# Turning the routed rows of six experts by DMA transposes of two-byte planes, with gates and weight loads moved behind them

## The chip, the cores and the metric

The kernel runs on one core of a Trainium2 chip, as one launch. The metric is the device time of an execution in microseconds, as a median of several runs; lower is better. The kernel before takes 338.1 us (three runs: 337.73, 338.10 and 340.49).

## The reference, cut to what matters

Two layers follow each other, all in float32.

- A gated recurrent attention over 768 steps for 4 batches of 8 heads of width 40. It gives `x`, a matrix of 3072 tokens by 320 features.
- A mixture of 8 experts with one expert per token. `logits = normalize(x) @ normalize(emb).T / tau`; each token goes to its largest logit, and its gate is the softmax share of that logit. Then, for each expert `e` and the tokens sent to it:

```
h = np.maximum(x[mask] @ w1[e], 0.0)                 # 320 -> 1024
out[mask] = gate_w[mask, None] * (h @ w2[e])         # 1024 -> 320
```

`w1` is 8 x 320 x 1024 and `w2` is 8 x 1024 x 320. The change touches only the expert layer, from the point where the token lists of all experts are known.

## The kernel before, in words

The order of the work is written out by hand: every engine takes its instructions in the order of the program, and closures in lists (`todo`, `xps`, `early`) say after which matrix product the next small piece of other work is put into the engines' queues. The DMA queue of SyncE (SP) issues the plain loads and stores in that order too; POOL issues the indirect ones.

**Precision.** Each float32 operand of a matrix product is split into a high and a low part (`xh`/`xl`, `w1h`/`w1l`, `hh`/`hl`, `w2h`/`w2l`), and a product is three matmuls. The last 64 features of `x` stand in one tile `xt`, high parts in partitions 64 to 127 and low parts in 0 to 63.

**The lists.** Attention output rows lie in DRAM as `x_d`, 336 floats a row: 320 features and the gate. The first two experts have special treatment: their first 256 rows each are gathered while attention still runs, and their second 256 rows ("b" in tile names) follow. The other six are sorted by size (`arrange`, line 217) and get lists of at most 448, 448, 384, 384, 320 and 320 rows (`CAPS`). An expert of these six is a pass `e` of the loop at line 1480, `e` from 2 to 7, with `j = e - 2`.

**One pass.** `mm1` (line 366) makes one of 8 blocks of the hidden layer: 8 matmuls into a PSUM tile `ph` (three of them exist), a ReLU on ACT into `hh`, a subtraction on DVE into `hl`. `mm2` (line 385) makes up to 128 output rows: 24 matmuls into a PSUM tile `po` (two exist), multiplied by the gate on DVE into `ob`, and scattered to `out` by an indirect DMA of POOL. For a list that ends in 64 rows, the last block takes 16 matmuls, a copy on ACT and two operations on DVE.

**What a pass prepares for the next one.** While pass `e` computes, pass `e + 1` is made ready:

- `load` (line 166) asks for the seven raw weight pieces, three of `w1` (512, 512 and twice 256 KB) and four of `w2` (320 KB each), on the SP queue. There are seven buffers `raw`, so a load waits until the piece of the expert before it in that buffer is split. All seven are put into the SP queue at the start of the pass.
- `piece` (line 186) splits a raw piece: a copy on ACT, a subtraction on DVE. One piece follows each `mm1` and two follow each `mm2`.
- `gather` (line 313) fetches the rows of the list into `xs`, 128 rows per indirect DMA of POOL, also at the start of the pass (the lists of `j` = 0 and 1 earlier).
- `x_chunk` (line 332) turns the rows. For each of three chunks of 128 features, TensorE transposes the three or four blocks of rows into one PSUM tile `pt`; ACT and DVE split it into `xh`/`xl` or `xt`. The first chunk is turned after the first `mm2`, the other two after the second. For the first of the six lists the three chunks follow the first three `mm2` of the "b" rows.
- `row_gates` (line 316) copies the gates of the list from `xs` at the start of its own pass.

**Before the loop.** The "b" rows go through 16 `mm1` of 256 rows (8 for each of the two experts) and 4 `mm2`. Beside the first of them run the small DVE steps of `arrange` (`ranks`, `places`, `lists`, `beyond`). `where` (line 1440) reads the sorted order into SP registers and puts all seven loads of expert 2 into the queue; `tokens` (line 1448) gathers the first list.

Of the kernel before, what the change touches and what calls it, by code (L numbers as in the profile page):

```python
# [11 lines left out]
F32 = mybir.dt.float32  # L12
# [2 lines left out]
F16 = mybir.dt.float16  # L15
I32 = mybir.dt.int32
U32 = mybir.dt.uint32
AF = mybir.ActivationFunctionType
ALU = mybir.AluOpType
AX = mybir.AxisListType  # L20
# [3 lines left out]
E, F = 8, 1024  # L24
NT = B * S
DM = H * D
P = 128
L = 64
# [6 lines left out]
CAP = 512  # L35
NTT = CAP // P
# [4 lines left out]
NE = 2  # L41
# [4 lines left out]
CAPS = (448, 448, 384, 384, 320, 320)  # L46
TILES = [[slice(a, min(a + P, n)) for a in range(0, n, P)] for n in CAPS]
# [21 lines left out]
def tile_mlstm_moe(  # L69
# [22 lines left out]
    V, G, A, T, SY = nc.vector, nc.gpsimd, nc.scalar, nc.tensor, nc.sync  # L92
# [5 lines left out]

    y_d = dr.tile([S, B * H, D], F32, name="y_d", tag="y_d")
    x_d = dr.tile([NT + 1, XW], F32, name="x_d", tag="x_d")  # L100
    left_d = dr.tile([E, NS, P, 1], I32, name="left_d", tag="left_d")
    oe_d = dr.tile([E, 1], I32, name="oe_d", tag="oe_d")

# [209 lines left out]
    def gather(cols):  # L313
        return gather_rows(lp.tile([P, NTT, XW], F32, name="xs", tag="xs"), cols)

    def row_gates(xs, n):

        gt = mp.tile([P, NTT], F32, name="gt", tag="gt")
        for a in range(0, n, P):
            r = min(P, n - a)  # L320
            V.tensor_copy(gt[0:r, a // P : a // P + 1], xs[0:r, a // P, DM:XC])
        return gt
# [9 lines left out]
    def x_chunk(x, xs, c, w=CAP):  # L332
        xh, xl, xt = x
        pt = pM.tile([P, 512], F32, name="pt", tag="pm")[:, 0:w]
        f = (0, P, DM - P)[c]
        for a in range(0, w, P):
            r = min(P, w - a)
            T.transpose(pt[:, a : a + r], xs[0:r, a // P, f : f + P], ident[0:r, 0:r])  # L338
        if c < 2:
            A.copy(xh[:, c, 0:w], pt)  # L340
            V.tensor_tensor(xl[:, c, 0:w], pt, xh[:, c, 0:w].bitcast(F32), ALU.subtract)
        else:
            A.copy(xt[L:P, 0:w], pt[L:P])
            V.tensor_tensor(xt[0:L, 0:w], pt[L:P], xt[L:P, 0:w].bitcast(F32), ALU.subtract)
# [21 lines left out]
    def mm1(ws, x, xc, f, hs, hc):  # L366
        w1h, w1l, (xh, xl, xt) = ws["w1h"], ws["w1l"], x
        fs = slice(f * P, (f + 1) * P)
        ph = pH.tile([P, 512], F32, name="ph", tag="ph")[:, 0 : xc.stop - xc.start]
        ops = [(w[:, c, fs], xh[:, c, xc]) for c in range(2) for w in (w1h, w1l)]  # L370
        ops += [(w1h[:, c, fs], xl[:, c, xc]) for c in range(2)]
        ops += [(w[:, 2, fs], xt[:, xc]) for w in (w1h, w1l)]
        for i, (lt, rh) in enumerate(ops):
            T.matmul(ph, lt, rh, start=i == 0, stop=i == len(ops) - 1)  # L374
        hh, hl = hs[0][f][:, hc], hs[1][f][:, hc]
        A.activation(hh, ph, AF.Relu)  # L376
        w = hc.stop - hc.start
        m = w - w % P
        V.scalar_tensor_tensor(hl[:, 0:m], ph[:, 0:m], 0.0, hh[:, 0:m].bitcast(F32), ALU.max, ALU.subtract)  # L379
        if m < w:  # L380
            V.scalar_tensor_tensor(
                hs[0][f][:, w : 2 * w - m], ph[:, m:w], 0.0, hh[:, m:w].bitcast(F32), ALU.max, ALU.subtract
            )
# [94 lines left out]
    with ExitStack() as actx:  # L478
# [711 lines left out]
        w_loads, exps = [], {}  # L1190
# [127 lines left out]
        def do(k):  # L1318
            for _ in range(k):
                if todo:  # L1320
                    todo.pop(0)()
# [56 lines left out]
        def first_out(i, po, ob=None):  # L1378
            mm2_out(po, xs_a[:, i // HT, i % HT, DM:XC], ida_v[i], f"a{i}", ob)
# [43 lines left out]

    exps[1]["tiles"](w22[1], 2)
    xs = gather(slots_b)
    todo += [exps[1]["piece"](*p) for p in PIECES2]
    while early:
        work(1, 2)
# [6 lines left out]
    first_outs = [(None, ob0), (None, ob1), (po2,), (po3,)]  # L1435

    gt_b = row_gates(xs, CAP)
    at = []

    def where():  # L1440

        at.extend(
            nc.values_load(order[0:1, j : j + 1], engines=[ET.SP], min_val=0, max_val=E - 1) for j in range(NO)
        )
        exps[2] = load_expert(2, at[0])
        todo[:] += [exps[2]["load"](i) for i in range(7)]

    def tokens():
        nonlocal xs
        xs = gather(ids_v[0])  # L1450

    ranks, places, lists, beyond = arrange(mp)
    todo += ranks + places + [where] + lists + [tokens]
    hs = hidden("b")
    for e in range(NE):
        for f in range(FC):
            mm1(exps[e]["ws"], xp, slice(e * HALF, (e + 1) * HALF), f, hs, slice(e * HALF, (e + 1) * HALF))
            do(3 - e)
            if f % 4 == 1:
                first_out(2 * e + f // 4, *first_outs[2 * e + f // 4])  # L1460
        if e == 0:
            exps[2]["tiles"](wp, 1)
            todo += beyond
    xp = x_tiles(mp, "2", CAP)
    xps = [lambda c=c: x_chunk(xp, xs, c, CAPS[0]) for c in range(3)]
    todo += [exps[2]["piece"](*p) for p in PIECES1]
    for i in range(NE * HT):
        e, a = divmod(i, HT)
        mm2(exps[e]["ws"], hs, slice(i * P, (i + 1) * P), gt_b[:, i : i + 1], slots_b[i], f"b{i}")
        if i == 1:  # L1470
            xs_n = gather(ids_v[1])
        if i == HT - 1:
            exps[2]["tiles"](w22[0], 2)
            todo += [exps[2]["piece"](*p) for p in PIECES2]
        do(3 if i < HT else 4)
        if xps:
            xps.pop(0)()
    while todo:
        do(1)
    for e in range(NE, E):  # L1480
        j = e - NE
        ws, x, w = exps[e]["ws"], xp, slice(0, CAPS[j])
        xps = []
        gt = row_gates(xs, CAPS[j])
        if e + 1 < E:
            exp = exps[e + 1] = load_expert(e + 1, at[j + 1])
            exp["tiles"](wq if e % 2 == 0 else wp, 1)
            exp["tiles"](w22[(e + 1) % 2], 2)
            todo += [exp["load"](i) for i in range(7)]
            todo += [exp["piece"](*p) for p in PIECES1 + PIECES2]  # L1490
            n = CAPS[j + 1]
            xs = gather(ids_v[j + 1]) if j else xs_n
            xp = x_tiles(mp, e + 1, CAP)
            xps = [lambda c=c, xp=xp, xs=xs, n=n: x_chunk(xp, xs, c, n) for c in range(3)]
            do(7)
        hs = hidden(e)
        for f in range(FC):
            mm1(ws, x, w, f, hs, w)
            do(1)
        for i, a in enumerate([0, len(TILES[j]) - 1, *range(1, len(TILES[j]) - 1)]):  # L1500
            t = TILES[j][a]
            mm2(ws, hs, t, gt[0 : t.stop - t.start, a : a + 1], ids_v[j][a], f"{e}_{a}")
            for _ in range(1 + (i == 1)):
                if xps:
                    xps.pop(0)()
            do(2)
        while todo:
            do(1)
        while xps:
            xps.pop(0)()  # L1510
# [209 lines left out]
```

## Time and profile before

| | |
|---|---|
| median of three runs | 338.1 us |
| profiled execution | 339.62 us, of which the span of the trace is 337.9 |
| TensorE (PE) busy | 313.2 us, 93% of the span |
| DVE, ACT, POOL busy | 223.3, 161.6 and 148.7 us |
| share of PE in the chain that ended last | 80% |
| mean granted TensorE clock | 0.968 of full speed |
| PE and clock from 192 to 330 us | busy all 138 us, clock 1.00 |

A matmul's length in the trace overlaps the next one's, so the pace of TensorE is read from the distance of two starts, or from the chain of waits, which gives each group only the time by which it moved the end. A row of the chain is: start, length, engine, names, line, count. In a timeline a row is: start, length, engine, line, operation, what it writes and reads, and in brackets the idle time before it and what ended that. "SPq" is the SP queue, and the time of such a row is that of the issue, not of the transfer. In a table by window, each engine has its busy time in the window with the instruction count, and at the end stand the granted clock, the busy share of the 16 DMA engines and GB/s.

### The profile page before, as it was taken

Reading aid. Unit: us, or ns where it says so; the run is one execution under the profiler, and the core shown is the slowest. Engines: PE = TensorE matmul, PEld = TensorE weight load, DVE = VectorE, ACT = ScalarE, POOL = GpSimd, SP = SyncE. Lnnn points to the kernel's source line nnn. Section 1 sums busy time; section 2 is a strip of 40 time slices with the busy share of each in tenths; the row PEclk is TensorE's granted clock in tenths of the full one; section 3 lists DMA queues with packets and bytes.
Section 4 is the critical chain, followed back from the end, with each engine's and each line's share of the span. In section 5 each row is a group of like instructions: output and inputs, shape, how many; then the busy total and the mean of one; then the engine's idle time right before and its main releaser. Section 6 shows DMA issues by size and latency. Waiting matters only on the chain.

```text
span 337.9 us, 9698 instructions
## 1 busy us (share of the span) xinstructions
PE 313.2 (93%) x3697; PEld 293.4 (87%) x3697; DVE 223.3 (66%) x644; ACT 161.6 (48%) x416; POOL 148.7 (44%) x183
## 2 busy tenths in 40 slices
PE   7859998989988999989699999999999999999992
PEld 3848897888977889989699999999999999999992
DVE  6776787897995679846336594566666684675520
ACT  6584654645654584533144363354454372554310
POOL 7775676667777387232423501250340231322112
PEclk9797999999999799999879999999999999999997
DMA  5896698999996541120871966437348458330001
GB/s 157 296 308 218 200 276 282 261 273 264 283 299 175 180 136 39 23 71 22 243 226 45 296 205 181 127 101 224 108 138 210 125 175 193 94 99 29 21 19 38
DMA packets 31610, 56.24 MB, mean 166 GB/s; under 512 B 6970, under 2 KB 21510, under 8 KB 31554
## 3 DMA queue, kind: packets, MB, share of 16 engines
q1 hardware_dynamic: 28738, 47.08, 47.7%
q0 software_dynamic: 2560, 8.35, 8.3%
q8 instruction: 31, 0.51, 0.6%
q14 instruction: 25, 0.20, 0.2%
q10 hardware_dynamic: 256, 0.10, 0.1%
HBM read 47.51 MB, written 8.39 MB: 165 GB/s over the span
## 4 chain that ended last, share of the span: by engine, by line
PE 80%; DMA 7%; DVE 4%; issue 3%; ACT 2%; another core or an unknown queue 1%; POOL 1%; POOLq 0%; SPq 0%
PE ph L374 28%; PE po L406 17%; PE s L571 5%; PE po_b L406 4%; PE y L652 4%; PE y L663 3%; PE po_a L406 3%; DMA kv_s<-in_kv 3%; PE c L610 3%; PE po L391 3%; PE pt L338 3%; PE pm L729 2%; DMA kq_s<-in_kq 2%; PE px L715 2%; DMA en<-in_emb 1%
## 5 line engine op out<-in xcount | busy, mean ns | idle before, releaser
L425 POOL DMA_INDIRECT out<-ob,ids x20 | 19.7, 985 | 102.7 <-DVE ob L422 86.4
L376 ACT ACTIVATE hh<-ph 128x448 fp32r<-128x448 f32 (+2 forms) x48 | 23.6, 491 | 45.4 <-PE ph L374 24.8
L406 PE MATMUL po<-w2h,hh 128*128 128x320 f32 x128 | 40.3, 314 | 0.0
L406 PE MATMUL po<-w2h,hl 128*128 128x320 f32 x128 | 39.6, 309 | 0.0
L406 PE MATMUL po<-w2l,hh 128*128 128x320 f32 x128 | 39.6, 309 | 0.0
L556 POOL TENSOR_TENSOR uv<-kv_s,u_t 64x328 f32<-64x328 f32 x47 | 34.8, 740 | 7.3 <-DMA kv_s<-in_kv 2.7
L379 DVE SCALAR_TENSOR_TENSOR hl<-ph,hh 128x384 fp32r<-128x384 f32 (+1 forms) x48 | 24.5, 511 | 15.5 <-ACT hh L376 11.8
L374 PE MATMUL ph<-xh,w1h 128*128 128x448 f32 (+2 forms) x96 | 32.1, 337 | 0.0
L571 PE MATMUL s<-kq_s 128*64 128x64 f32 x768 | 29.2, 231 | 3.1 <-DVE w_s L580 1.6
L374 PE MATMUL ph<-xh,w1l 128*128 128x448 f32 (+2 forms) x96 | 32.0, 336 | 0.0
L571 PEld LDWEIGHTS s<-kq_s 128*64 128x64 f32 x768 | 26.8, 145 | 4.7 <-DVE w_s L580 2.5
L195 ACT CAST w1h<-raw 128x512 fp32r<-128x512 f32 x48 | 28.9, 613 | 0.0
L422 DVE TENSOR_SCALAR ob<-po,gt 128x320 f32<-128x320 f32 x16 | 8.8, 551 | 28.9 <-PE po L406 28.9
L198 DVE TENSOR_TENSOR w2l<-raw,w2h 128x320 fp32r<-128x320 f32 x58 | 27.1, 503 | 0.2
L699 POOL TENSOR_TENSOR x<-x,sig 128x320 f32<-128x320 f32 x21 | 18.2, 865 | 17.9 <-DMA kq_s<-in_kq 5.6
L652 PE MATMUL y<-uv,w_s 128*64 128x82 f32 x384 | 25.2, 247 | 0.2 <-issue 0.2
L195 ACT CAST w2h<-raw 128x320 fp32r<-128x320 f32 x62 | 25.2, 458 | 0.1
L374 PE MATMUL ph<-xl,w1h 128*128 128x448 f32 (+2 forms) x96 | 24.5, 336 | 0.0
L198 DVE TENSOR_TENSOR w1l<-raw,w1h 128x512 fp32r<-128x512 f32 x36 | 24.4, 686 | 0.0
L406 PEld LDWEIGHTS po<-w2h,hh 128*128 128x128 f32 x128 | 24.0, 188 | 0.3
L406 PEld LDWEIGHTS po<-w2l,hh 128*128 128x128 f32 x128 | 24.1, 188 | 0.0
L406 PEld LDWEIGHTS po<-w2h,hl 128*128 128x128 f32 x128 | 24.0, 188 | 0.0
(312 smaller groups left out, 921.3 us busy)
## 6 DMA issues: line engine op xcount, KB each, us to landing
raw<-in_w SPq DMA_DIRECT2D x32, 320.0 KB
kv_s<-in_kv SPq DMA_DIRECT2D x24, 324.0 KB
kq_s<-in_kq SPq DMA_DIRECT2D x48, 160.0 KB
raw<-in_w SPq DMA_DIRECT2D x14, 512.0 KB
raw<-in_w SPq DMA_DIRECT2D x18, 256.0 KB
sig<-in_og SPq DMA_DIRECT2D x24, 160.0 KB
x_d<-x SPq DMA_DIRECT2D x24, 160.0 KB
raw<-in_w SPq DMA_DIRECT2D x4, 128.0 KB
```

The source lines that it names most:

```text
L195: A.copy(h, src)
L198: (eng or V).tensor_tensor(lo, src, h.bitcast(F32), ALU.subtract)
L338: T.transpose(pt[:, a : a + r], xs[0:r, a // P, f : f + P], ident[0:r, 0:r])
L374: T.matmul(ph, lt, rh, start=i == 0, stop=i == len(ops) - 1)
L376: A.activation(hh, ph, AF.Relu)
L379: V.scalar_tensor_tensor(hl[:, 0:m], ph[:, 0:m], 0.0, hh[:, 0:m].bitcast(F32), ALU.max, ALU.subtract)
L406: T.matmul(po[0 : ts_.stop - ts_.start, 0:DM], lt[f][:, ts_], rh[:, f], start=k == 0, stop=k == len(ops) - 1)
L425: store = G.indirect_dma_start(out=out, out_offset=bass.IndirectOffsetOnAxis(ap=slots, axis=0), in_=ob, in_offset=None, bounds_check=NT - ...
L556: eng.tensor_tensor(uv[n % NB][rows, :, :, r], list(rows_of(n))[1][rows], u_t[rows, j, b].unsqueeze(3).broadcast_to([L, 2, NP, D1]), ALU.mult,
L571: T.matmul(s[r * L : r * L + L, c, p], k_of(n, odd)[:, a, cs], q_of(n)[:, a, cs], start=True, stop=True,)
L652: T.matmul(yh[c][:, g, :, odd], w_s[n % NB][:, c, 2 * g + odd], uv[n % NB][:, c, 2 * g + odd], start=g + odd == 0, stop=n < B and c == 0, ...
L699: eng.tensor_tensor(x_of(n), x_of(n), sigs[j][:, b].rearrange("p (h d) -> p h d", h=H), ALU.mult)
```

## The change

- `x_chunk` is no longer used for the six lists. A function `turn` makes the steps for one list: `part` copies 128 rows on POOL from `xs` into `halves`, pulling the two 16-bit halves of each float apart into two planes of 384 columns (320 used, the rest zero); `go` copies the gates on DVE, stores the planes to DRAM (`x2_d`, one or two DMAs), and then issues one transposing DMA from `x2_d` into `turned`, where the two halves of a float come to lie side by side again. All these DMAs are on the SP queue.
- `split` makes `xh`, `xl` and `xt` from `turned` with two steps: `rows` (the first 256 features in one ACT copy and one DVE subtraction) and `rest`.
- In pass `e`, `part` and `go` follow one `mm1` each. The loads of the next `w2` come behind `go`, one after each further `mm1` or `mm2`; those of the next `w1` stay at the start of the pass. The splits of `w2` follow the `mm2` only. `rows` and `rest` follow the first and second `mm2`.
- The rows of the list after next are gathered after the first `mm2` of a pass.
- For the first list, the parts follow the "b" `mm1` of the second expert from its second block on, `go` and the `w2` loads come behind, and `rows` and `rest` follow the second and third `mm2`. `where` comes behind `tokens`, and the three `w1` loads are put between the steps of `beyond`.

```diff
+    def turn(xs, j):
+        n, full = CAPS[j], CAPS[j] // P
+        def part(a):
+            r = min(P, n - a * P)
+            G.tensor_copy(halves[0:r, a, :, 0:DM], xs[0:r, a, 0:DM].bitcast(U16).rearrange("p (d h) -> p h d", h=2))
+        def go():
+            gts[j] = row_gates(xs, n)
+            SY.dma_start(
+                x2_d[0 : 2 * full * P].rearrange("(a p h) d -> p a (h d)", p=P, h=2),
+                halves[:, 0:full].rearrange("p a h d -> p a (h d)"),
+            )
+            if n > full * P:
+                SY.dma_start(
+                    x2_d[2 * full * P : 2 * n].rearrange("(p h) d -> p (h d)", h=2),
+                    halves[0 : n - full * P, full].rearrange("p h d -> p (h d)"),
+                )
+            SY.dma_start_transpose(
+                out=turned.rearrange("p c t -> p (c t)").bitcast(U16).rearrange("p (c t) -> p c t", c=3)[:, :, 0 : 2 * n],
+                in_=x2_d[0 : 2 * n],
+            )
+        later = [exps[j + NE]["load"](i) for i in range(3, 7)]
+        return [lambda a=a: part(a) for a in range(len(TILES[j]))] + [go] + later
+    def split(x, n):
+        xh, xl, xt = x
+        def rows():
+            A.copy(xh[:, :, 0:n], turned[:, 0:2, 0:n])
+            V.tensor_tensor(xl[:, :, 0:n], turned[:, 0:2, 0:n], xh[:, :, 0:n].bitcast(F32), ALU.subtract)
+        def rest():
+            A.copy(xt[L:P, 0:n], turned[0:L, 2, 0:n])
+            V.tensor_tensor(xt[0:L, 0:n], turned[0:L, 2, 0:n], xt[L:P, 0:n].bitcast(F32), ALU.subtract)
+        return [rows, rest]
...
-        todo[:] += [exps[2]["load"](i) for i in range(7)]
...
-    todo += ranks + places + [where] + lists + [tokens]
+    todo += ranks + places + lists + [tokens, where]
+    for i in range(3):
+        todo += [lambda i=i: exps[2]["load"](i)(), *beyond[3 * i : 3 * i + 3]]
...
+            if e and f and turns:
+                turns.pop(0)()
...
+            G.memset(halves[:, :, :, DM:], 0)
+            turns = turn(xs, 0)
...
-            todo += [exp["load"](i) for i in range(7)]
-            todo += [exp["piece"](*p) for p in PIECES1 + PIECES2]
+            exp["load"](0)()
+            exp["load"](1)()
+            turns = turn(xs, j + 1)
+            todo += [exp["load"](2)] + [exp["piece"](*p) for p in PIECES1]
...
-            xs = gather(ids_v[j + 1]) if j else xs_n
-            xps = [lambda c=c, xp=xp, xs=xs, n=n: x_chunk(xp, xs, c, n) for c in range(3)]
-            do(7)
+            xps = split(xp, n)
...
             mm1(ws, x, w, f, hs, w)
+            if turns:
+                turns.pop(0)()
             do(1)
+        if e + 1 < E:
+            todo += [exp["piece"](*p) for p in PIECES2]
...
+            if i == 0 and e + 2 < E:
+                xs = gather(ids_v[j + 2])
```

## Rows read from the trace of the kernel before

**Rows 1.** The table by window, 192 to 330 us, in the columns described above.

```profile
192.00:330.00 138.00, 138.00 (x868) 133.86 (x867) 86.17 (x213) 61.96 (x137) 32.05 (x32) 1.00 0.47 131
```

**Rows 2.** The chain of waits, from expert 2's first `mm1` on.

```profile
191.05 13.03 PE ph L374 x64
...
207.59 0.53 PE pt L338 x4
208.12 2.54 PE po L391 x16
210.66 1.21 PE pt L338 x8
...
219.10 12.97 PE ph L374 x64
...
235.59 0.33 PE pt L338 x3
235.92 2.35 PE po L391 x16
238.27 0.66 PE pt L338 x6
...
245.97 11.10 PE ph L374 x64
...
292.06 9.40 PE ph L374 x64
...
304.98 0.42 PE pt L338 x3
...
307.95 0.99 PE pt L338 x6
...
312.65 9.39 PE ph L374 x64
```

**Rows 3.** Groups of POOL by shape: line, operation, shapes, count, busy, mean ns.

```profile
L198 POOL TENSOR_TENSOR w1l<-raw,w1h 128x512 fp32r<-128x512 f32 x12 | 15.3, 1286 | 5.5 <-ACT w1h L195 4.3 <-DMA x_d<-x 1.1
...
L1016 POOL MEMSET uv<- 128x656 f32 x1 | 0.6, 636 | 0.0
```

**Rows 4.** Timeline of POOL: the last gather of the first list, and two scatters.

```profile
162.97 0.96 POOL L297 DMA_INDIRECT xs<-x_d,ids  x1 [0.30 <-issue]
...
168.89 1.00 POOL L425 DMA_INDIRECT out<-ob_a,ids_a  x1 [3.62 <-DVE ob_a L422]
...
219.97 0.98 POOL L425 DMA_INDIRECT out<-ob,ids  x1 [2.54 <-DVE ob L422]
```

**Rows 5.** Issue of an 88 KB store of 64-byte runs; GB/s, 137 to 142 us in 40 slices.

```profile
137.54 0.39 SPq L472 DMA_DIRECT2D x_d<-sw  x1
...
GB/s 0 0 0 0 0 0 0 0 0 0 0 15 93 84 87 87 85 85 84 86 16 0 0 0 0 131 0 0 0 0 0 0 0 0 0 0 0 0 0 0
```

**Rows 6.** GB/s from 182 to 190 us in 40 slices, beside weight loads.

```profile
GB/s 0 0 0 0 0 0 0 0 0 0 0 0 0 82 164 102 164 266 266 266 328 451 396 375 430 410 451 430 369 369 348 348 367 224 129 237 142 196 183 204
```

**Rows 7.** Groups of ACT and DVE from 176 to 338 us: the splits of the weights.

```profile
L195 ACT CAST w1h<-raw 128x512 fp32r<-128x512 f32 x35 | 21.2, 614 | 0.0
...
L198 DVE TENSOR_TENSOR w1l<-raw,w1h 128x512 fp32r<-128x512 f32 x36 | 24.4, 686 | 0.0
L198 DVE TENSOR_TENSOR w2l<-raw,w2h 128x320 fp32r<-128x320 f32 x48 | 21.5, 484 | 0.2
```

**Rows 8.** Timeline of SP, ACT and PE beside the loads of expert 2.

```profile
166.23 2.09 SPq L179 DMA_DIRECT2D raw<-in_w  x4
166.34 0.94 ACT L376 ACTIVATE hh_b<-ph 128x256 fp32r<-128x256 f32 x3 [3.28 <-remote]
...
167.24 0.58 PE L374 MATMUL ph<-xh_p,w1h 128*128 128x256 f32 x1 [2.44 <-DVE hl_b L379]
```

**Rows 9.** The table by window, 163 to 173 us.

```profile
163.00:167.00 4.00, 1.34 (x10) 1.01 (x8) 0.67 (x2) 0.72 (x4) 1.96 (x2) 0.89 0.98 317
167.00:173.00 6.00, 5.76 (x27) 5.76 (x28) 3.22 (x15) 1.28 (x5) 1.00 (x1) 0.50 0.99 286
```

More of the change, by code (lines that the diff above doesn't have):

```diff
@@ L17 @@
 U32 = mybir.dt.uint32
+U16 = mybir.dt.uint16
 AF = mybir.ActivationFunctionType
@@ L100, in tile_mlstm_moe @@
     x_d = dr.tile([NT + 1, XW], F32, name="x_d", tag="x_d")
+    x2_d = dr.tile([2 * CAP, 3 * P], U16, name="x2_d", tag="x2_d")
     left_d = dr.tile([E, NS, P, 1], I32, name="left_d", tag="left_d")
@@ L1425, in tile_mlstm_moe @@
     xs = gather(slots_b)
+    halves = lp.tile([P, NTT, 2, 3 * P], U16, name="halves", bufs=1)
+    turned = lp.tile([P, 3, CAP], F32, name="turned", bufs=1)
     todo += [exps[1]["piece"](*p) for p in PIECES2]
@@ L1437, in tile_mlstm_moe @@
     gt_b = row_gates(xs, CAP)
-    at = []
+    at, gts = [], {}
+    def turn(xs, j):
[29 more added lines that the diff above has]
+        return [rows, rest]
     def where():
@@ L1460, in tile_mlstm_moe @@
                 first_out(2 * e + f // 4, *first_outs[2 * e + f // 4])
+            if e and f and turns:
+                turns.pop(0)()
         if e == 0:
             exps[2]["tiles"](wp, 1)
-            todo += beyond
+            G.memset(halves[:, :, :, DM:], 0)
+            turns = turn(xs, 0)
     xp = x_tiles(mp, "2", CAP)
-    xps = [lambda c=c: x_chunk(xp, xs, c, CAPS[0]) for c in range(3)]
+    xps = split(xp, CAPS[0])
     todo += [exps[2]["piece"](*p) for p in PIECES1]
@@ L1474, in tile_mlstm_moe @@
             todo += [exps[2]["piece"](*p) for p in PIECES2]
+        if turns:
+            turns.pop(0)()
+        if 0 < i < 3:
+            xps.pop(0)()
         do(3 if i < HT else 4)
-        if xps:
-            xps.pop(0)()
     while todo:
         do(1)
+    xs = xs_n
     for e in range(NE, E):
@@ L1482, in tile_mlstm_moe @@
         ws, x, w = exps[e]["ws"], xp, slice(0, CAPS[j])
-        xps = []
-        gt = row_gates(xs, CAPS[j])
+        xps, turns, gt = [], [], gts[j]
         if e + 1 < E:
@@ L1498, in tile_mlstm_moe @@
             mm1(ws, x, w, f, hs, w)
+            if turns:
+                turns.pop(0)()
             do(1)
+        if e + 1 < E:
+            todo += [exp["piece"](*p) for p in PIECES2]
         for i, a in enumerate([0, len(TILES[j]) - 1, *range(1, len(TILES[j]) - 1)]):
@@ L1502, in tile_mlstm_moe @@
             mm2(ws, hs, t, gt[0 : t.stop - t.start, a : a + 1], ids_v[j][a], f"{e}_{a}")
-            for _ in range(1 + (i == 1)):
-                if xps:
-                    xps.pop(0)()
+            if turns:
+                turns.pop(0)()
+            if i == 0 and e + 2 < E:
+                xs = gather(ids_v[j + 2])
+            if xps:
+                xps.pop(0)()
             do(2)
```

## The prediction

> **What bounds the kernel now.** I read the page first (PE is busy for 93% of the span), then the table by window. From expert 2's first block to expert 7's end TensorE is busy without a break at full clock [rows 1]; no other engine is above 63% there. So in this stretch a TensorE instruction taken out shortens the run by its pace, and anything new costs nothing until TensorE waits for it. The chain of waits gives the pace of each group and the length of each pass [rows 2]. The stretch just ahead, 163 to 173 us, is different: ACT gets its ReLU 3.28 us late, released by an unknown queue, TensorE stands for 2.44 us and then has half its clock [rows 8, 9].
>
> **What is removed.** The six lists' transposes leave TensorE. In the chain, four transposes that end in a 64-row block take 0.53 us and eight 1.21; three and six full ones take 0.33 and 0.66; three and six that end in 64 rows 0.42 and 0.99 [rows 2]. After a 64-row block the next group is slower: 16 matmuls take 2.54 us, against 2.35 after full ones, so 0.19 for the switch [rows 2]. First list, three times four: 3 x (0.53 + 0.19) = 2.16. Second: 0.53 + 1.21 + 2 x 0.19 = 2.12. The two lists of 384: 0.99 each. The two of 320: 0.42 + 0.99 + 0.38 = 1.79 each. Sum **9.8 us**, all on the path. Their splits from PSUM leave ACT and DVE too and come back as `rows` and `rest`, of the same number of elements.
>
> **What is added.** For each list a serial chain: parts on POOL, the store, the turning DMA, the split. Nobody on TensorE waits for it before the next expert's first `mm1`. In the working below T0 is the first `mm1` of a pass; numbers are for 448, 384 and 320 rows.
>
> Start of the parts. POOL still has the scatter of the pass before; in pass 3 it ends at 219.97 + 0.98, which is T0 + 1.9 [rows 2, 4]. The rows were gathered a pass earlier, so they are no wait.
>
> Parts. No 16-bit copy stands in the trace. One copy moves 640 elements; a fill costs 0.97 ns an element, a two-input subtraction 2.5 [rows 3], so 0.6 to 1.6 us. A copy has one input and one strided read; I take 1.2, the middle. Four, three and three copies: 4.8, 3.6, 3.6.
>
> Store. 688, 590 and 492 KB in runs of 1,536 bytes. A small store is done 2.0 us after the start of its issue (137.54 to the end of the plateau at 139.5), and runs of 64 bytes move at 85 GB/s [rows 5]; weight loads reach about 400 [rows 6]. The runs are nearer the loads, so I take 300 GB/s: 0.4 issue + 2.0 + data = 4.7, 4.4, 4.0. With 85 GB/s it would be up to 5.8 more.
>
> Turning. No trace shows it. Between the same two rates the data take 1.7 to 8.1 us at 448 rows; with 2.0 of fixed time 3.7 to 10.1. Its source rows are 768 bytes long, between both but nearer the loads, so I take 3 us of data: T = 5.0, 4.6, 4.1. Its writes are two bytes wide across partitions, which is why the slow end stays open (second rival).
>
> Split. `rows` has 896 elements a partition: on DVE 686 + 384 x (686 - 484)/192 = 1,090 ns, on ACT at most 614 x 896/512 = 1,074 [rows 7]. With `rest` 2.8, 2.4, 2.0.
>
> Without T the chain ends at T0 + 14.2, 12.3 and 11.5. Pass lengths without transposes, from the starts in [rows 2]: 28.05 - 2.12 = 25.9 for pass 2, 25.9 for pass 3, 43.3/2 = 21.7 for passes 4 and 5, 18.8 for pass 6. So T may be 11.7 for the second list (made in pass 2), 13.6 and 9.4 for the lists of 384, 10.2 and 7.3 for those of 320, before TensorE waits. With my T five lists are hidden with 3 us or more.
>
> The first list is tight. Its last gather is issued by 163.9, but POOL reaches the parts behind a scatter that ends at 169.9 [rows 4]. 169.9 + 4.8 + 4.7 + 5.0 + 2.8 = 187.2, and three splits of `w1` stand on DVE between `rows` and `rest`: 3 x 0.69 [rows 7] = 189.3. Without its transposes expert 2 would start at 191.05 - 2.16 = 188.9: a wait of **0.4 us**.
>
> **Waits that queue others.** The store holds SP until the parts are done, and the turning DMA holds it until the store has landed; behind it stand only four `w2` loads (1.28 MB, 4 to 5 us at 300 GB/s). In pass 6 they land by about T0 + 18.5; their eight splits at 0.48 on DVE, done as they land, end near 19.5, before the first ReLU of the next pass at 20. Three `ph` tiles give 3 x 1.17 us more. If `rows` is put into ACT and DVE before the data are there, the following `ob` waits; the second `po` tile covers one `mm2`, 24 x 2.35/16 = 3.5 us [rows 2]. The gathers, four of about 1 us [rows 4], now sit between two scatters of POOL; three `ob` tiles cover them. Moving the gates and the order of `where` and `tokens`: nothing; they are the same short instructions, and the gates are copied well ahead of their use.
>
> **The burst.** At 163 to 173 us TensorE loses 4.00 - 1.34 = 2.7 us to idling and half of 5.8 to the clock, 5.6 in all [rows 9]. The change takes four of the seven loads out of this burst. But the first of these four was issued at 166.23, when ACT had already waited since 163.06 [rows 8]; so I give back nothing here, with 5.6 as the bound of the gain. If it went, the first list would have to come earlier as well and would take part of it back.
>
> **Sum.** 339.62 - 9.8 + 0.4 = 330.2 for the profiled execution; it lies 1.5 above the median of the three runs, so against the median **328.7**.
>
> **A rule that speaks against it.** In [rows 2] a transpose costs TensorE 0.11 to 0.18 us in the stream. The Trainium skill (VectorE: DVE Perf Modes, The three transpose paths) lists 390 ns for a 128 x 128 block of two bytes on TensorE and 1,309 ns on the DMA crossbar, and advises TensorE wherever a PSUM destination will do. If blocks went one after the other, 21 of them would be an estimate of 27.5 us for the first list, and the sum would end well above 338. The skill's Advanced Engine Details and Errata (X-Bar Transpose) says on the other hand that such DMAs are as fast as ordinary ones. No run here shows either yet.
>
> **Rivals.**
>
> 1. **Turning at the rate of small runs**, 85 GB/s [rows 5]: T = 10.1, 8.9, 7.8. The first list comes 5.1 later, the last misses its 7.3 by 0.5: 6.0 in waits, gain 3.8 to 4. Time **334**. For it: all 16-bit data. Against it: long source rows.
> 2. **Turning becomes the bound (slower).** The writes are two-byte columns; if the engines move them in pieces of half those 64 bytes at the same time per piece, the rate is 42 GB/s and T = 18.2, 15.9, 13.6. TensorE then waits ahead of every expert: 13.6 for the first list, then 6.5, 2.3, 6.5, 3.4 and 6.3, together 38.6. Time 338.1 - 9.8 + 38.6 = **367**. It decides below about 70 GB/s, where the waits reach 10 us. The crossbar rule of the skill, taken block by block, lands in this case.
> 3. **Bursts in every pass.** Store, turning and four loads now go back to back; if each makes ACT late as at 163 us, the cost is up to 5.6 in five passes: 338.1 - 9.8 + 28 = **356**. Against it: in the passes before, loads of this size already ran beside TensorE without a break [rows 1], with 47% of the DMA engines busy; twice 3.5 MB more (2304 rows of 1,536 bytes) against 131 GB/s x 138 us = 18 MB.
>
> **Chances.** Forecast 0.60 (323 to 332); rival 1, or something that eats as much, 0.18 (332 to 338), of which 0.08 lies within 1% of the time before; rival 2 0.15, with 0.04 near break-even; rival 3 0.07. A measurement of this kernel can tell about 1% from no change. Faster 0.60 + 0.10 = 0.70, same 0.12, slower 0.18. The range 323 to 338 holds the first two; its lower end is the gain with the burst gone.
>
> **What would show it.** In the changed profile: 12 transposes of `pt` in place of 72; passes of 25.9, 25.9, 21.7, 21.7 and 18.8 us; TensorE without a break from expert 2 on; the ACT copy from `turned` not waiting, or waiting for the DMA by less than 3 us. The transposing DMA should land within 4 to 10 us of its issue, and POOL's copies take 0.6 to 1.6 us. I am wrong if `xh` of an expert waits for `turned` with TensorE idle behind it, if the gap at 163 us goes, or if ACT waits for the late `w2` pieces longer than the `ph` tiles cover.

## The result, and the profile after

The changed kernel takes **328.75 us** (median of four runs, 328.52 to 333.67), the kernel before 339.11 beside it (four runs): a ratio of 0.9717, 95% interval 0.9664 to 0.9771. Some executions of either kernel fall into a slower state; ratios and intervals, here and below, are of the others alone and so are not the quotients of the medians. The profiled execution took 328.59 us, its span is 326.8 where it was 337.9.

The page says that TensorE lost 10.5 us of busy time (313.2 before) and kept its share, while POOL gained 19.6 us (148.7 before); the 3.5 MB more written to HBM (11.93 MB, 8.39 before) are the planes (2304 rows of 1,536 bytes):

```profile
PE 302.7 (93%) x3637; PEld 285.8 (87%) x3637; DVE 224.3 (69%) x638; ACT 161.8 (49%) x410; POOL 168.3 (52%) x204
```

The chain of waits after, from the first product of the b rows on, answers to [rows 2]:

```profile
172.25 14.08 PE po_b L408 x96
186.34 2.59 PE ph L376 x8
...
189.42 2.43 DVE w2l L200 x4
...
192.07 0.54 DVE hl L381
...
192.90 8.34 PE ph L376 x40
...
204.76 2.35 PE po L393 x16
...
214.15 12.97 PE ph L376 x64
...
240.03 11.10 PE ph L376 x64
...
261.68 11.12 PE ph L376 x64
...
283.35 9.43 PE ph L376 x64
...
302.17 9.39 PE ph L376 x64
```

No `pt` stands in it any more, `po` L393 runs at 2.35 everywhere instead of 2.54, and the starts of passes 3 to 7 give lengths of 25.9, 21.7, 21.7 and 18.8 us, as forecast. The one new thing is in pass 2: `ph`, four subtractions of `w2` on DVE, a `hl`, and only then `ph` again.

The table by window answers to [rows 9] and [rows 1]:

```profile
163.00:167.00 4.00, 1.26 (x9) 1.01 (x8) 1.09 (x5) 1.07 (x4) 2.42 (x3) 1.00 0.96 306
167.00:173.00 6.00, 5.79 (x47) 5.79 (x48) 3.87 (x14) 2.49 (x7) 4.60 (x6) 1.00 0.64 193
192.00:320.00 128.00, 127.11 (x803) 125.56 (x804) 83.73 (x200) 60.03 (x128) 46.74 (x46) 1.00 0.63 183
```

The burst at 163 us is still there (TensorE busy for 1.26 of 4.00 us, 1.34 before), but the clock behind it is 1.00 where it was 0.50: 2.5 us that the prediction had not counted on. The last row starts inside the wait of pass 2; without that wait TensorE is unbroken to the end.

Measured from the first `mm1` of each stretch to the next one, in TensorE's timeline (us):

| | b rows | pass 2 | pass 3 | pass 4 | pass 5 | pass 6 |
|---|---|---|---|---|---|---|
| before | 37.52 | 28.06 | 26.86 | 22.64 | 23.46 | 20.59 |
| forecast, from pass 2 on | | 25.9 | 25.9 | 21.7 | 21.7 | 18.8 |
| after | 32.88 | 27.82 | 25.88 | 21.64 | 21.68 | 18.82 |

The span went down by 11.1: 4.6 in the b rows (2.16 of transposes, 2.5 of clock), 0.2 in pass 2 (2.1 of transposes less 1.9 of new wait), 1.0, 1.0, 1.8 and 1.8 in passes 3 to 6, and 0.7 outside these columns.

The timelines of SP, ACT, DVE, POOL and PE after, at the first two lists (a row is read as in [rows 8]):

```profile
171.30 0.41 SPq L1454 DMA_DIRECT2D x_d<-halves  x1
171.96 0.54 SPq L1459 DMA_DIRECT2D x_d<-halves  x1
174.93 2.93 SPq L1463 DMA_TRANSPOSE turned<-x_d  x1
...
197.22 3.94 SPq L1463 DMA_TRANSPOSE turned<-x_d  x1
...
180.52 0.94 ACT L1476 CAST xh<-turned 128x896 fp32r<-128x896 f32 x1 [6.30 <-DMA turned<-x_d]
...
203.32 0.94 ACT L1476 CAST xh<-turned 128x896 fp32r<-128x896 f32 x1 [1.50 <-DMA turned<-x_d]
...
188.95 0.55 DVE L424 TENSOR_SCALAR ob_b<-po_b,gt 128x320 f32<-128x320 f32 x1 [1.66 <-PE ph L376]
189.42 2.73 DVE L200 TENSOR_TENSOR w2l<-raw,w2h 128x320 fp32r<-128x320 f32 x4
...
190.77 1.95 POOL L1450 COPY halves<-xs 128x640 uint16<-128x640 uint16 x2
...
192.90 0.44 PE L376 MATMUL ph<-xh,w1h 128*128 128x448 f32 x1 [1.70 <-DVE hh L383]
```

From the turning's issue to ACT's copy it is 5.6 us at 174.93 and 6.1 at 197.22. The store takes 3.6 from its issue to that of the turning. And four `w2l` take 2.73 us here where [rows 7] give 4 x 0.484; two of them last 0.48 us and the two that run beside POOL's copies 1.00. Ahead of them DVE stands idle for 1.66 us: the last `ob_b` of the b rows waits for TensorE until 2.8 us into pass 2.

The queries of the tile `turned` and of POOL's groups (minimum, median and maximum in ns; then idle time of the engines before it) give the rest:

```profile
L1463 SPq DMA_TRANSPOSE turned<-x_d x6: 1549/2254/3938, 174.9 to 290.7; - x6
...
  DMA turned<-x_d: 9.3, 3
```

```profile
L1450 POOL COPY halves<-xs 128x640 uint16<-128x640 uint16 x16 | 12.0, 788 | 0.2 <-DMA xs<-x_d,ids 0.2
```

ACT waited for a turning three times of six, 9.3 us in all; a full copy on POOL takes 0.79 us.

### The profile page after: what moved, and what is told of

Same layout as the page of the kernel before. It is cut to its first block, busy times and chain, and to the rows that moved or that the text cites. A ratio compares the mean times of both kernels' runs of the same rounds, so it can differ in the third digit from the quotient of the medians.

```text
span 326.8 us, 9615 instructions
## 1 busy us (share of the span) xinstructions
PE 302.7 (93%) x3637; PEld 285.8 (87%) x3637; DVE 224.3 (69%) x638; ACT 161.8 (49%) x410; POOL 168.3 (52%) x204
## 3 DMA queue, kind: packets, MB, share of 16 engines
HBM read 47.51 MB, written 11.93 MB: 182 GB/s over the span
## 4 chain that ended last, share of the span: by engine, by line
PE 76%; DVE 10%; DMA 5%; issue 3%; ACT 3%; POOL 1%; POOLq 0%; SPq 0%; DVEq 0%
PE ph L376 28%; PE po L408 17%; PE s L573 5%; PE po_b L408 4%; PE y L654 4%; PE po_a L408 3%; PE c L612 3%; PE po L393 3%; DMA kv_s<-in_kv 3%; PE y L665 3%; PE pm L731 2%; DMA sig<-in_og 2%; DVE op L896 1%; PE px L717 1%; DVE w_s L582 1%
## 5 line engine op out<-in xcount | busy, mean ns | idle before, releaser
L427 POOL DMA_INDIRECT out<-ob,ids x20 | 22.9, 1145 | 79.2 <-DVE ob L424 70.6
L408 PE MATMUL po<-w2h,hh 128*128 128x320 f32 x128 | 39.5, 309 | 0.0
L200 DVE TENSOR_TENSOR w2l<-raw,w2h 128x320 fp32r<-128x320 f32 x58 | 28.1, 531 | 0.6
L612 PE MATMUL c<-uv,kv_s 128*40 128x82 f32 x352 | 24.1, 250 | 2.6 <-issue 1.5
L197 ACT CAST w2h<-raw 128x320 fp32r<-128x320 f32 x62 | 24.4, 457 | 3.2 <-DMA raw<-in_w 2.9
L654 PE MATMUL y<-uv,w_s 128*64 128x82 f32 x384 | 25.7, 250 | 0.0
L628 ACT COPY c_mid<-c 40x164 f32<-40x164 f32 x48 | 14.0, 292 | 23.2 <-PE c L612 22.7
L299 POOL DMA_INDIRECT xs<-x_d,ids x20 | 21.9, 1095 | 6.2 <-issue 5.8
L200 DVE TENSOR_TENSOR w1l<-raw,w1h 128x512 fp32r<-128x512 f32 x36 | 25.1, 706 | 0.0
```

The source lines that it names most:

```text
L197: A.copy(h, src)
L200: (eng or V).tensor_tensor(lo, src, h.bitcast(F32), ALU.subtract)
L299: G.indirect_dma_start(out=xs[0 : c.shape[0], a], out_offset=None, in_=x_d[0:rows], in_offset=bass.IndirectOffsetOnAxis(ap=c, axis=0), bou ...
L408: T.matmul(po[0 : ts_.stop - ts_.start, 0:DM], lt[f][:, ts_], rh[:, f], start=k == 0, stop=k == len(ops) - 1)
L427: store = G.indirect_dma_start(out=out, out_offset=bass.IndirectOffsetOnAxis(ap=slots, axis=0), in_=ob, in_offset=None, bounds_check=NT - ...
L612: T.matmul(pc[odd * L : odd * L + D, 2 * g : 2 * g + 2], k_rows[:, c, p], uv[n % NB][:, c, p], start=False, stop=g == 1, skip_group_check= ...
```

## The experiments

They ran in three sets, each beside its own runs of the kernel before, and are compared within a set: that kernel's median was 338.72 us in the first (e1 to e4), 333.73 in the second (e5 to e8) and 333.45 in the third (e9 to e12).

**e1: the order alone.** Gathers, gates and loads in the new order, the rows turned on TensorE as before:

```
-    xps = split(xp, CAPS[0])
+    xps = [lambda c=c, xp=xp, xs=xs: x_chunk(xp, xs, c, CAPS[0]) for c in range(3)]
...
         def part(a):
-            r = min(P, n - a * P)
-            G.tensor_copy(halves[0:r, a, :, 0:DM], xs[0:r, a, 0:DM].bitcast(U16).rearrange("p (d h) -> p h d", h=2))
+            pass
...
-            SY.dma_start_transpose(
```

> The new order of gathers, gates and weight loads alone; the six lists are turned on TensorE again, as before. Theory (the gain is the 9.8 us of transposes taken off a TensorE that never waits): 336 to 340 us, as before, with 72 transposes in the trace; at most 2.4 us better if the half clock at 166 us stays away. Rival (the order of the loads is what helped): 329 to 333 us.

Measured: 341.25 us, ratio 1.0003 (0.9942 to 1.0063). The passes are 28.00, 26.86, 22.64, 23.46 and 20.58 us, those of before to 0.1. The order is worth nothing by itself. (Here and in e2 the gathers of the later lists come one `mm2` later than in the changed kernel.)

**e2: the transposes put back beside the DMA route.** The changed kernel, with the 60 transposes also issued on TensorE, into PSUM that nobody reads:

```
+    def refill(c, xs, n):
+        pt = pM.tile([P, 512], F32, name="pt", tag="pm")[:, 0:n]
...
+            T.transpose(pt[:, a : a + r], xs[0:r, a // P, f : f + P], ident[0:r, 0:r])
```

> The changed kernel with the 60 transposes put back on TensorE, at their old places, into a PSUM tile that nobody reads; the rows still come from the DMA. Theory: 328.8 + 9.8 = 338.5 us, down to 337 where a transpose fills the wait of pass 2 (1.7 us). Rival (TensorE's time is not what was won): below 333 us.

Measured: 338.42, ratio 1.0009 (0.9950 to 1.0068); passes 28.00, 26.87, 22.64, 23.45, 20.58. The whole gain goes with 60 TensorE instructions, and with them the wait of pass 2. The DMA route itself cost nothing.

**e3: each turning issued twice.**

```
+            SY.dma_start_transpose(
+                out=turned.rearrange("p c t -> p (c t)").bitcast(U16).rearrange("p (c t) -> p c t", c=3)[:, :, 0 : 2 * n],
+                in_=x2_d[0 : 2 * n],
+            )
```

> Every transposing DMA is issued twice into the same tile, the second behind the first, so that turning takes 8 to 12 us in place of 4.1 to 6.1. Theory (five lists are hidden with 3 us or more, the first has no slack): only the first list comes late, by 4 to 6 us, the last by about 1: 333 to 336 us, passes 3 to 5 of the same length. Rival A (turning is on the path of every pass): 28 us more, about 357. Rival B (there is slack everywhere): below 330.

Measured: 340.98, ratio 1.0096 (1.0050 to 1.0142), 5 us above what the theory had said and far below rival A. The passes are 34.24 (b rows), 30.92, 26.08, 21.67, 22.30 and 22.45, and the end after the start of pass 7 is 27.2 long (24.7 to 25.7 in the runs with one turning). Timelines of SP, ACT and PE:

```profile
176.59 3.70 SPq L1463 DMA_TRANSPOSE turned<-x_d  x1
182.24 2.74 SPq L1467 DMA_TRANSPOSE turned<-x_d  x1
...
295.34 0.40 SPq L1454 DMA_DIRECT2D x_d<-halves  x1
...
301.62 1.79 SPq L1463 DMA_TRANSPOSE turned<-x_d  x1
305.78 1.66 SPq L1467 DMA_TRANSPOSE turned<-x_d  x1
...
187.73 0.94 ACT L1480 CAST xh<-turned 128x896 fp32r<-128x896 f32 x1 [10.23 <-DMA turned<-x_d]
...
296.26 0.39 PE L376 MATMUL ph<-xh,w1h 128*128 128x320 f32 x1 [2.16 <-DVE hh L383]
```

The distances give T for each size: 5.6 and 5.5 us at 448 rows here, 4.2 and 4.0 at 320. The first list came some 5.5 us later, as expected: ACT copies it 11.1 us behind the first turning's issue, not 5.6. TensorE waits 1.96 us for its `xt`, and with a mean clock of 0.80 around that wait pass 2 is 3.1 longer than after. The b rows are 1.4 longer, but not by the list, which nobody on TensorE needs there: the granted clock was 0.82 and 0.89 in the two stretches of 6 us from 165 us on, where it was 1.00 after. Passes 3 to 5 took up 4 to 6 us more of turning for 0.8 in all. What nobody had expected is the end. The four `w2` loads stand behind the second turning, so TensorE waits 2.16 at the start of pass 6 for what DVE does late; the next store then took 6.3 us from 295.34 to the turning at 301.62, where it takes 3.6 after at the first list, and the last list came late. So four of the five later lists have 4 us to spare for the turning, and the SP queue behind a turning is what runs out first, in the short passes.

**e4: the first list on TensorE, the other five by DMA.**

```
-            turns = turn(xs, 0)
+            turns = [exps[2]["load"](i) for i in range(3, 7)]
...
-    xps = split(xp, CAPS[0])
+    xps = [lambda c=c, xp=xp, xs=xs: x_chunk(xp, xs, c, CAPS[0]) for c in range(3)]
```

> The first of the six lists is turned on TensorE as before, the other five by DMA. Theory (the 1.7 us for which TensorE stands in pass 2 come from the first list's late split, which keeps ACT and DVE from the weight splits): 2.2 us more for the transposes, 1.7 less for the wait: 328.5 to 330 us, no wait in pass 2. Rival (the wait comes from POOL's copies beside DVE's subtractions): the wait stays, 330.5 to 331.5 us.

Measured: 333.90, ratio 0.9863 (0.9817 to 0.9910). As a time it missed the expectation: the b rows of its profile are 36.38 long with the clock low behind the burst. The step it was made for came out. Pass 2 is 26.54 long, 1.28 shorter than after, and TensorE's wait in it fell from 1.70 to 0.43, though DVE's four `w2l` are as slow as after (PE and DVE timelines of e4; POOL's copies run beside from 195.16):

```profile
197.28 0.44 PE L376 MATMUL ph<-xh,w1h 128*128 128x448 f32 x1 [0.43 <-DVE hh L383]
...
193.34 0.55 DVE L424 TENSOR_SCALAR ob_b<-po_b,gt 128x320 f32<-128x320 f32 x1 [2.74 <-PE po_b L408]
193.81 2.73 DVE L200 TENSOR_TENSOR w2l<-raw,w2h 128x320 fp32r<-128x320 f32 x4
```

DVE stands idle for 2.74 us ahead of the last `ob_b` here, so no queue is left behind the first list. That fits the theory, but it does not prove it against the profile after: there the last `ob_b` came 2.8 us into pass 2 and here 1.5, and this difference alone is as large as the 1.28. TensorE also has its 2.16 us of transposes back, which gives DVE that much more time. The cleaner test is e6.

**e5: the changed kernel again**, nothing edited, in the second set.

> The changed kernel itself once more, as the measure for the three beside it on the same chip. 328 to 331 us; passes 2 to 6 of 27.8, 25.9, 21.6, 21.7 and 18.8 us.

Measured: 326.42 (322.85 to 331.02), ratio 0.9812 (0.9749 to 0.9876). There is no burst here at all: the b rows take 29.44, and ACT's ReLUs come every 0.96 us. Pass 2 is 27.58, the others 25.88, 21.65, 21.67 and 18.78. The wait for `hl` in pass 2 is only 0.63 here, with the same program (DVE, POOL and PE timelines of e5):

```profile
184.00 1.69 DVE L200 TENSOR_TENSOR w2l<-raw,w2h 128x320 fp32r<-128x320 f32 x4
...
184.37 2.18 POOL L427 DMA_INDIRECT out<-ob_b,ids_b  x1 [1.49 <-DMA xs<-x_d,ids]
186.55 3.18 POOL L1450 COPY halves<-xs 128x640 uint16<-128x640 uint16 x4
...
186.43 0.44 PE L376 MATMUL ph<-xh,w1h 128*128 128x448 f32 x1 [0.63 <-ACT hh L378]
```

POOL's scatter takes 2.18 us here and 0.98 after, so its copies start behind the four subtractions, which take 1.69. What makes the scatter short or long is not shown. (The row of PE names ACT's `hh`, but in e5, e10 and e11 the wait ends 0.15 us behind DVE's last operation on the first block, as it does after.)

**e6: expert 2's `w1` split first.** All six of its pieces behind the first product of the b rows, so that DVE has done them before the turning lands:

```
-        do(3 if i < HT else 4)
+        do((6, 2, 3, 3)[i])
```

> All six w1 splits of expert 2 follow the first mm2 of the b rows, ahead of the split of the turned rows, in place of three ahead and three between its two halves; so ACT and DVE work while they wait for the turning DMA. Theory (the 1.7 us in pass 2 come from DVE falling behind the late first list): DVE is 2 us earlier, pass 2 falls from 27.8 to 26 us, 1.5 us faster than the changed kernel. Rival (POOL's copies slow DVE's subtractions just then): pass 2 stays above 27 us.

Measured: 323.95, ratio 0.9748 (0.9676 to 0.9820). Pass 2 is 26.51, 1.07 less than in e5. By time e6 and e5 overlap; the step shows in the trace (PE timeline of e6):

```profile
186.90 0.44 PE L376 MATMUL ph<-xh,w1h 128*128 128x448 f32 x1 [0.32 <-DVE hh L383]
```

**e7: the sorted order reaches SP later.** A guess at what makes ACT late at 163 us:

```
-            V.tensor_copy(order, key)
+            V.tensor_copy(order_f, key)
...
-    todo += ranks + places + lists + [tokens, where]
+    todo += ranks + places + lists + [tokens] + beyond + [order_late, where]
```

> The sorted order reaches SP 2.8 us later, behind the steps of beyond, so that the loads of expert 2 start at about 165 us in place of 162.5; the gathers stay. Theory A (the loads make ACT late at 161 to 167 us): the 3 us for which TensorE stands move to about 164 to 170. Theory B (it is something in the order of ACT's own instructions or the gathers): they stay at the eighth and ninth mm1 of the b rows. Time 328 to 332 either way.

Measured: 330.25, ratio 0.9848 (0.9783 to 0.9913). Inconclusive on the burst: nothing in this set shows it, so there was none to take away. But pass 2 is 28.79 long, 1.21 more than in e5: the turning is issued 5.4 us behind the second part of the store (3.9 in e5), and TensorE waits 1.73 us for the first list's `xt`.

**e8: the `w2` loads ahead of the store and the turning.**

```
+        def ahead(a):
+            later[a]()
+            part(a)
...
-        return [lambda a=a: part(a) for a in range(len(TILES[j]))] + [go] + later
+        return [lambda a=a: ahead(a) for a in range(k)] + [rest_go]
```

> The four w2 loads of a pass are asked for ahead of the store and the turning DMA, not behind them. Theory (the order on the SP queue matters only to the first list, which has no slack): its rows come 3 to 4 us later behind 1.3 MB, passes 3 to 6 keep their lengths: 330 to 333 us. Rival A (weights behind the turning are what keeps it hidden): every list late, above 340. Rival B (no matter): as the changed kernel.

Measured: 333.41, ratio 1.0009 (0.9965 to 1.0053): the whole gain is gone. Timelines of SP, ACT and PE, then the table by window:

```profile
170.62 0.54 SPq L1459 DMA_DIRECT2D x_d<-halves  x1
178.36 4.16 SPq L1463 DMA_TRANSPOSE turned<-x_d  x1
...
185.82 0.94 ACT L1487 CAST xh<-turned 128x896 fp32r<-128x896 f32 x1 [14.20 <-DMA turned<-x_d]
...
186.81 0.74 PE L376 MATMUL ph<-xh,w1h 128*128 128x448 f32 x1 [4.02 <-ACT xh L1487]
```

```profile
180.00:186.80 6.80, 2.79 (x20) 2.53 (x18) 0.01 (x1) 0.98 (x2) 2.21 (x3) 1.00 0.77 178
186.80:197.00 10.20, 8.75 (x23) 7.29 (x24) 10.08 (x20) 6.66 (x15) 4.94 (x6) 0.50 0.73 214
```

With 1.28 MB of loads ahead of it the turning is issued 7.7 us behind the second part of the store (3.9 in e5; 3.0 after, 171.96 to 174.93), and ACT copies 7.5 us behind that (5.0 in e5, 5.6 after). TensorE stands for 4.02 us and then runs at half clock for 10: the b rows take 33.62 us, pass 2 takes 31.62, together 8.2 more than in e5. Passes 3 to 6 are 25.88, 21.65, 21.67 and 18.81: in them the order of these loads does not matter. Behind the first list it is worth all of the gain.

**e9 and e10: before and after, profiled side by side in the third set.**

> The kernel before, profiled on this chip, to stand beside the next three. The ReLU of block 11 or 13 of the b rows came 3 us late in the profiles of before, of the changed kernel and of the first four experiments, and in none of the second four. Theory: whether it comes late hangs on the execution or the chip, not on the change; then this profile and the next three show the same (all late, the first pass about 37.5 us long here and 33 to 36 in the next three; or none, 31.5 here and 29.5 there). Rival: the change moves it; then it is late here and not in the next three.

> The changed kernel, as the reference of the next run on the same chip. If POOL's copies of the second list start while DVE takes the last four low parts of w2, those four take 2.7 us and TensorE then waits 1.7 us in pass 2; if they start behind them, 1.7 us and a wait of 0.6.

Measured: 333.78 and 324.74, one run each. The kernel before shows no burst here either (the table by window of e9, to be held against [rows 9]):

```profile
163.00:167.00 4.00, 4.00 (x35) 4.00 (x35) 3.21 (x14) 1.57 (x5) 3.08 (x4) 1.00 0.89 287
```

So the burst comes and goes with either kernel, and this pair, without it on both sides, is the cleanest account of the change:

| | b rows | pass 2 | pass 3 | pass 4 | pass 5 | pass 6 | sum |
|---|---|---|---|---|---|---|---|
| e9, before | 31.60 | 28.00 | 26.87 | 22.64 | 23.45 | 20.58 | 153.14 |
| e10, after | 29.44 | 28.07 | 25.88 | 21.65 | 21.67 | 18.78 | 145.49 |
| difference | -2.16 | +0.07 | -0.99 | -0.99 | -1.78 | -1.80 | -7.65 |
| transposes as forecast | -2.16 | -2.12 | -0.99 | -0.99 | -1.79 | -1.79 | -9.84 |

Every list gives what was forecast, and pass 2 alone takes 2.2 back.

**e11: the second list's copies on ACT.**

```
-            G.tensor_copy(halves[0:r, a, :, 0:DM], xs[0:r, a, 0:DM].bitcast(U16).rearrange("p (d h) -> p h d", h=2))
+            (A.copy if j == 1 else G.tensor_copy)(halves[0:r, a, :, 0:DM], xs[0:r, a, 0:DM].bitcast(U16).rearrange("p (d h) -> p h d", h=2))
```

> The changed kernel with the four two-byte copies of the second list alone taken by ACT in place of POOL. Theory: POOL's copies slow DVE's subtractions of w2 that run beside them, and that delay is the larger half of the wait in pass 2; with the copies on ACT the last four low parts of w2 take 1.7 us again and pass 2 is 26.5 to 27 us long where it is 27.8 with POOL, unchanged where POOL's copies came behind the subtractions anyway. Rival: the wait is only the queue of late splits; then the four take 2.7 us still or the wait stays 1.7. ACT's own copies, some 0.7 us each between ReLUs, may delay a ReLU by 0.3 to 0.7. Passes 3 to 6 unchanged in both.

Measured: 324.59 us, ratio 0.9812 (0.9716 to 0.9907). Pass 2 is 27.42, 0.65 less than in e10, but 0.4 above what was expected. The timelines of DVE, POOL and PE in e10:

```profile
179.24 1.09 DVE L1477 TENSOR_TENSOR xl<-turned,xh 128x896 fp32r<-128x896 f32 x1 [3.47 <-ACT xh L1476]
...
185.42 2.73 DVE L200 TENSOR_TENSOR w2l<-raw,w2h 128x320 fp32r<-128x320 f32 x4
186.77 2.61 POOL L1450 COPY halves<-xs 128x640 uint16<-128x640 uint16 x3
188.90 0.44 PE L376 MATMUL ph<-xh,w1h 128*128 128x448 f32 x1 [1.67 <-ACT hh L378]
```

and of DVE, POOL and PE in e11:

```profile
183.59 1.69 DVE L200 TENSOR_TENSOR w2l<-raw,w2h 128x320 fp32r<-128x320 f32 x4
...
183.96 2.18 POOL L427 DMA_INDIRECT out<-ob_b,ids_b  x1 [1.49 <-DVE ob_b L424]
...
186.03 0.44 PE L376 MATMUL ph<-xh,w1h 128*128 128x448 f32 x1 [0.57 <-ACT hh L378]
```

Against e10 the four subtractions take 1.69 us instead of 2.73, and the wait behind them falls from 1.67 to 0.57, by the same 1.1. But the edit need not have done this. POOL's scatter takes 2.18 us in this execution, as in e5, so copies on POOL would have come behind the subtractions anyway; and e5, with its copies on POOL, has the same 1.69, a wait of 0.63 and a pass 2 only 0.16 longer. So the executions of one program (after and e10 against e5 and e7) show that the subtractions are slow when the copies run beside them; e11 agrees, and does not settle it by itself. Where the copies did run beside DVE in e5, on the next two subtractions of `w1`, these take 1.03 and 1.89 us, and 0.69 each in e11. What is left of the wait is the queue of late splits; in e5 and e11 a wait for the first list's `xt` comes on top (0.41 and 0.24).

**e12: e6 once more**, in the third set.

> The changed kernel with all six splits of expert 2's w1 put after the first product of the b rows, on another chip. Theory: pass 2 is 26.5 us long, 1.1 to 1.3 shorter than with the changed kernel, and the passes behind it are unchanged: 25.9, 21.6, 21.7, 18.8. Rival: the first time's 1.1 us was due to that chip; then pass 2 is 27.5 or longer.

Measured: 325.80, ratio 0.9828 (0.9751 to 0.9905). Pass 2 is 26.85, 1.22 less than in e10, the others as there. The gain of the trace repeats (the unedited kernel's pass 2 is 27.58 to 28.07 long in its three profiles, e6's and e12's are 26.51 and 26.85); as a time it can't be told from e10 and e11, because the start of the b rows, which none of this touches, lies anywhere from 149.8 to 153.8 us in these two sets. So e6 is the better kernel by the trace, and no time shown here proves it.

## Why the prediction came out, step by step

**What is removed: right.** 9.8 us, list by list to 0.1 (e9 and e10), and e2 shows that the gain goes when these 60 instructions come back.

**The parts, the store and the turning: right in their place, the sum a little dear.** A copy takes 0.79 us, not 1.2 (the first list's four take 2.70). The store takes 3.6 us in the profile after and, for the first list, 4.9 in e10 and 5.5 in e5, where 4.7 stood. The 2.0 us of fixed time in that 4.7 already held the issue and the data of the small store, and 0.4 of issue was added once more. The turning takes 5.0 to 6.1 us at 448 rows where 5.0 stood (5.6 and 6.1 after, 5.1 and 5.8 in e10, 5.0 twice in e5), and 4.0 to 4.2 at 320 where 4.1 stood. From its first part to ACT's copy the first list takes 11.3 us after, 12.0 in e10 and 12.6 in e5; the forecast was 14.5.

The Trainium skill's rule that spoke against the change (VectorE: DVE Perf Modes, The three transpose paths) is not borne out: taken block by block it made an estimate of 27.5 us, and 5.0 to 6.1 were measured, so the blocks of one large turning do not follow one another at that price. Its other rule (Advanced Engine Details and Errata, X-Bar Transpose: as fast as ordinary DMAs) comes close: the same 688 KB take 3.6 us as a store and 5.6 as a turning in the profile after.

**Five lists hidden: right.** ACT waits for `turned` three times of six, and TensorE does not wait for one in passes 3 to 6. e3 shows the room: twice the T is still nearly hidden in passes 3 to 5.

**The first list tight: right, and its price failed.** The prediction looked for 0.4 us ahead of expert 2's first `mm1`. That wait is at most 0.4 with the loads where the change puts them (none after and in e10, 0.24 in e11, 0.41 in e5). ACT's wait for the turning, forecast below 3 us, is 6.30 after and 7.57 in e10 at this list, but TensorE does not feel it there. The step that failed is the next one. I had `rows` and `rest` of the first list taken by DVE with three splits of `w1` between them, and did not ask what else then stands in DVE's queue behind them. It is the eight subtractions of `w2`, ahead of the first `hl` of pass 2, and the `ph` tiles hold TensorE for three blocks only. Pass 2 is 1.7 to 2.2 us longer than the lengths forecast (after, e5 and e10). In e10 and e5 DVE has no pause from the subtraction of the turned rows to that `hl` (179.24 to 188.07 in e10), and e6 and e12 show that 1.1 to 1.2 of it goes when DVE does the `w1` splits earlier. In the profile after the queue is not the whole of it: DVE had done four of the eight by 187.3 and then stood for the last `ob_b`, and what made TensorE's release of that late is not known. Up to 1.1 of the stall comes and goes with POOL's copies beside DVE's subtractions (1.7 of wait after and in e10, 0.6 in e5 and e7); the pass itself moves by less, 0.5 between e10 and e5, as other waits come in. The prediction had costed POOL's copies as work on a free engine. The Trainium skill (SBUF — State Buffer, SBUF: two separate sides) says that VectorE and GpSimd share a pair of SBUF ports, and that an operation with two SBUF inputs and a GpSimd operation that reads SBUF lock each other out. The traces agree as far as they go: a subtraction of `w2` lasts 0.48 us alone and 1.00 beside the copies, while a full copy takes 0.98 beside them (1.95 for two) where the first list's four take 0.68 each. A lock and a shared rate would look alike in these rows.

**The burst gives back nothing: half wrong, by luck.** The gap stayed, as said. But in the profiled execution after, the clock did not fall behind it, which gave 2.5 us, nearly what pass 2 lost. The sum for the profiled execution was 330.2 and it came to 328.6: 2.5 less by the clock, some 0.6 less at the end, 1.5 more in front of and in pass 2. So the total was right partly because two errors cancel. Where no burst occurs in either kernel, the passes say 7.65 us and not 9.4, and the second set's ratio is 0.9812 (e5).

**The rivals.** Small-run rate: T would be 10.1 and is 5.0 to 5.6 for the first list. Turning as the bound: e3 doubles it and the whole gain is gone (1.0096 of the time before), so by this one test it decides from about twice the measured T; 1.4 us of e3's loss is clock in the b rows and not turning. Bursts in every pass: none, with the DMA engines 63% busy from 192 to 320 us instead of 47% [rows 1]. That the order of the loads counts as little as the prediction gave it (the loads "behind" cost nothing) is wrong for the first list: e8.

**Open.** What stops the work at 163 us in some executions. It showed in the profiles of before, after and e1 to e4, and in none of e5 to e12, in either kernel. e7 was meant to tell and could not. The prediction read it as ACT being late; in the profile after, ACT is the one that waits: its two late ReLUs are released by TensorE, after 2.64 and 2.71 us, and the first of them (163.22) starts 2.4 us behind the start of the last matmul of its block (160.84), where in e5 it is 0.3. So TensorE's release is late there, as it is for the last `ob_b` in pass 2. Why is not known. Nor is it settled why the clock fell behind it in the profile before and not in that after. The rows of PE and ACT after:

```profile
160.84 0.28 PE L376 MATMUL ph<-xt_p,w1l 128*128 128x256 f32 x1
...
163.22 0.38 ACT L378 ACTIVATE hh_b<-ph 128x256 fp32r<-128x256 f32 x1 [2.64 <-PE ph L376]
166.31 0.94 ACT L378 ACTIVATE hh_b<-ph 128x256 fp32r<-128x256 f32 x3 [2.71 <-PE ph L376]
```

## What to carry to other kernels

When work leaves the bounding engine for a chain of several others, cost not only the chain's end but what it pushes back in each queue that it passes: here the late first list moved weight splits on DVE in front of the next pass's first result. Turning a list by DMA takes 8 to 10.5 us here at 448 rows from the store to the copy on ACT (3.6 + 5.6 after, 5.5 + 5.0 in e5), and costs nothing where a pass has that much to spare; bulk loads put ahead of the first one, which has none, took the whole gain (e8). Compare step by step by the starts of the passes, not by the total: the total hid a gain of 2.5, a loss of 2 and a spread of 4 us in where the b rows start.

## What the runs showed of the hardware that was not expected

- A two-input subtraction of 128 x 320 on DVE lasts 0.48 us alone and 1.00 beside two-byte copies on POOL (after), one of 128 x 512 lasts 0.69 alone (e11) and 1.03 or 1.89 beside them (e5). A copy of the same kind takes ACT 0.71 us (e11).
- The same scatter of POOL beside the same subtractions took 0.98 us in some executions (after, e10) and 2.18 in others (e5, e7, e11); in the first the subtractions behind it were slow, in the second they were not.
- The issue of a turning DMA holds the SP queue for 1.5 to 3.9 us, that of a store 0.4 to 0.5 (after).
- A stall of TensorE did not always cost clock: with 1.26 of 4.00 us busy the granted clock stayed at 1.00 (2.4 GHz) after, and with 1.34 of 4.00 it fell to 0.50 (1.2 GHz) before; with 2.79 of 6.80 it fell to 0.50 for 10 us (e8).
- Behind 1.28 MB of loads a store of 688 KB held up the DMA that waits for it by 3.8 us or more (7.7 us from its second issue in e8, against 3.9 in e5, 3.5 in e10 and 3.0 after).
